# Half of pi filled last on VectorE, and the second k's read issued behind the operation that uses it

## The chip, the cores and the metric

The kernel runs on one core of a Trainium2 chip. The metric is device time in microseconds (us) of one execution; the times before are 218.34 us as the median of three runs (217.97 to 221.09). A core has five engines with an instruction queue each, executed in order: TensorE (PE, with PEld for its weight loads), VectorE (DVE), ScalarE (ACT), GpSimd (POOL) and SyncE (SP). ScalarE, GpSimd and SyncE also issue DMA transfers, which 16 DMA engines carry out.

## The reference

An attention block without softmax, followed by a token-mixing block.

```python
def phi(x):                                   # r = 8
    a = np.einsum('rd,bhsd->bhsr', S1, x)
    b = np.einsum('rd,bhsd->bhsr', S2, x)
    return np.einsum('bhsi,bhsj->bhsij', a, b).reshape(*x.shape[:-1], r * r)
q_p, k_p = phi(q), phi(k)                     # q, k, v: (4, 4, 1088, 32)
kv = np.einsum('bhsf,bhsd->bhfd', k_p, v)
z = np.sum(k_p, axis=2)
x = (q_p @ kv) / (q_p . z + 1e-06)            # heads joined: (4, 1088, 128)
...
theta = x @ w_theta
zr, zi = x * np.cos(theta), x * np.sin(theta)
y = einsum('ts,bsd->btd', w_tok_r, zr) + einsum('ts,bsd->btd', w_tok_i, zi)
u = x + y
return u + np.maximum(u @ w_ch, 0.0)
```

Here `@` and `.` in the line of `x` stand for the two einsums of the reference over the features. S1, S2 and the weights come as 64-bit numbers, and the kernel makes 32-bit numbers of them on chip.

## The kernel before

The work is cut into about 1,020 numbered operations, each a few instructions of one engine. The numbers are given in the order in which the program creates the operations; `ORDER` is a list, written out, of the order in which they are issued to their engines, and `STARTS` holds for each entry of `ORDER` a planned start in hundredths of a us. The starts decide only which buffer of a class is reused and how many idle matmuls (`spin`) TensorE runs between two operations. Each engine works through its own operations in this order; waits on semaphores between engines follow from the data.

A batch b has one read of k, q and v each (576 KB). The reads of k for b = 0 and 1 are issued by ScalarE (L668), all others by SyncE (L671), as are the rows of w_tok (L642, 1088 KB each), the small matrices S1 and S2 (`st`, L444 and L446) and a second copy of k for b = 1 to 3 (L714). Every read's completion is counted on one of eight counters, which are given to the reads in turn; a read whose counter is in use waits for the read that had it before.

What the start consists of, with the numbers that the change touches:

- 0 and 1: GpSimd fills `idle`, TensorE runs 39 idle matmuls.
- 2: VectorE fills the constants `halfpi`, `hm`, `bdm` and `ones` (`constants`, L414 to L422). They are used at different times: `halfpi` (half of pi in each partition, the bias that makes a sine a cosine) by operation 3 and then by L1203 from 54 us on.
- 3: ScalarE takes the sine of `halfpi` into `warm` (L433). The result isn't used; the sine's table is loaded by it ahead of need.
- 4 and 5: VectorE clears `st`, SyncE reads S1 and S2 into it. ScalarE (L459) and VectorE (the first L383 and L386) unpack them to `sp`; the scales, the block matrices `sbk` and the sketches of everything come from it.
- 29: ScalarE's read of k for b = 0 (k0). 32: ScalarE's read of k for b = 1 (k1), the "second k". 34, 33: SyncE's reads of k for b = 3 and b = 2. 30: SyncE's read of q for b = 0 (q0).
- ScalarE squares each k as it lands (L693, with an accumulated sum), VectorE rounds it (L383) and takes the rest (L379), TensorE transposes it (L790), and ScalarE copies the transposes out of PSUM (L793).

After the sketches, the rows of w_tok are unpacked (ScalarE L643 and L645, VectorE L383 and L379), the chain of small scales runs, and from about 57 us TensorE mixes tokens (L399 big,zs): b = 0 and 1 row by row, b = 2 and 3 together in seven products instead of eight.

In the order before, ScalarE's queue begins with the reads of k0 and k1, then the table load and `warm`, then the square of k0.

Of the kernel before, what the change touches and what calls it, by code (L numbers as in the profile page):

```python
# [31 lines left out]
RPS = 4  # L32
EARLY = (2, 60.0, 4.0)
ORDER = (
    29, 32, 4, 2, 5, 0, 1, 3, 34, 30, 356, 50, 33, 102, 44, 96, 6, 108, 103, 36, 7, 51, 366, 54, 144, 8, 97, 10, 9,
    11, 55, 109, 20, 52, 12, 57, 139, 58, 59, 60, 61, 62, 63, 126, 13, 31, 132, 56, 98, 127, 264, 14, 391, 128, 143,
    245, 15, 145, 64, 65, 67, 68, 78, 35, 69, 16, 70, 19, 148, 149, 150, 151, 152, 268, 99, 66, 79, 246, 53, 80, 100,
    110, 129, 17, 133, 130, 357, 25, 361, 81, 270, 83, 18, 203, 358, 359, 71, 41, 153, 104, 271, 210, 197, 351, 257,
# [39 lines left out]
    1013, 1007, 934, 938, 1014, 935, 1015, 939, 1016, 1017, 1018, 940, 1019, 941, 942, 943,  # L78
)
STARTS = (  # L80
    73, 73, 90, 92, 103, 130, 170, 220, 358, 404, 449, 458, 493, 510, 538, 546, 566, 579, 580, 584, 594, 612, 628,
    666, 802, 678, 693, 694, 706, 716, 719, 732, 752, 771, 798, 811, 812, 813, 815, 817, 819, 821, 823, 838, 830, 944,
    871, 899, 904, 918, 957, 967, 1088, 998, 1026, 1061, 1064, 1066, 1111, 1113, 1115, 1129, 1129, 1408, 1142, 1145,
    1155, 1164, 1168, 1170, 1172, 1174, 1176, 1225, 1236, 1251, 1251, 1260, 1271, 1299, 1303, 1313, 1319, 1327, 1334,
# [228 lines left out]
def kernel(  # L313
# [56 lines left out]
    V, A, G, T, SY = nc.vector, nc.scalar, nc.gpsimd, nc.tensor, nc.sync  # L370

    def fixed(shape, dt, name):
        b = Buf(None, shape, dt, name)
        n = math.prod(shape) * WORD[dt]
        b.ap = view(const.tile([P, (n + 3) // 4], F32, tag=name, name=name), shape, dt)
        return b
# [33 lines left out]
    halfpi = fixed((1,), F32, "halfpi")  # L410
    warm = fixed((1,), F32, "warm")

    def constants():
        V.memset(halfpi(), math.pi / 2.0)  # L414
        V.memset(hm(), 0.0)
        for h in range(H):
            V.memset(hm()[h * D:(h + 1) * D, h:h + 1], 1.0)
        V.memset(bdm(), 0.0)
        for h in range(H):
            j = h % 2  # L420
            V.memset(bdm()[j * 64:(j + 1) * 64, h:h + 1], 1.0)
        V.memset(ones(), 1.0)  # L422

    idle = fixed((GW,), BF16, "idle")
    nowhere = buf("ps", (GW,), F32, "nowhere")
# [4 lines left out]
    op("G", 0.3, lambda: G.memset(idle(), 0.0), [idle], [], due=-20.0)  # L430
    first = op("P", 3.2, lambda: [spin(112) for _ in range(39)], [nowhere], [idle], due=-10.0)
    op("V", 1.25, constants, [hm, bdm, halfpi, ones], [])
    op("A", 1.5, lambda: A.activation(warm(), halfpi(), AF.Sin), [warm], [halfpi], due=0.0)  # L433

# [1109 lines left out]
```

## Time and profile before

| what | value |
|---|---|
| runs | 217.97, 218.34, 221.09 us |
| profiled execution | 217.81 us, of which the instruction span is 215.9 us |
| busy, share of the span | PE 97%, PEld 71%, DVE 81%, ACT 53%, POOL 28% |
| chain that ended last | PE 63%, DMA 18%, ACT 14% |
| granted TensorE clock | 0.995 |
| DMA | 37.09 MB, mean 172 GB/s; 422 GB/s from 8 to 16 us |
| DMA share, 4 to 49 us | 1.02 |
| ScalarE's L668, issue to landing | 3.8 and 5.1 us |

Busy time is the time in which an engine executed something; a matmul's end is modelled, so a busy TensorE is not one at its peak. The chain is followed back from the last instruction, at each step to what released it. The DMA share is the mean busy share of the 16 DMA engines; it can pass 1 because packets overlap. A row of the timeline has start, duration, engine (with q for an instruction that only issues or waits), line, operation and tiles, and in brackets the idle time before it with what ended that.

### The profile page before, as it was taken

The page shows a single profiled execution, that of the slowest core. Times are in us where ns is not written, and L with a number is a line of the kernel's source. Part 1 is how long each engine was busy: PE and PEld are TensorE (multiplying, and loading weights), DVE is VectorE, ACT ScalarE, POOL GpSimd, SP SyncE. Part 2 cuts the span into 40 slices and gives each one's busy share as a digit, 9 for nine tenths or more (in the row PEclk, how much of TensorE's full clock was granted, in tenths as well). Part 3 has the DMA queues.
Part 4 walks back from the last instruction along what each step waited for, and adds up shares of the span by engine and source line. Part 5 has one row for each costly group of instructions (what it writes and reads, how often), then busy time and mean ns, then how long its engine had stood idle before and what let it go on. Part 6 is the DMA issues. An engine that isn't in the chain of part 4 may idle for free.

```text
span 215.9 us, 5832 instructions
## 1 busy us (share of the span) xinstructions
PE 208.9 (97%) x2396; PEld 152.8 (71%) x2396; DVE 174.3 (81%) x343; ACT 114.5 (53%) x256; POOL 59.7 (28%) x105
## 2 busy tenths in 40 slices
PE   7899999999999999999999999999999999999992
PEld 7677798868866666866668666667677776666781
DVE  1799998999999998999999798885994747456263
ACT  4899989999998895798704233363810000000000
POOL 1272740306400000604004100000006489950403
PEclk9999999999999999999999999999999999999998
DMA  6999999995998993192002402424050420010735
GB/s 222 395 418 419 384 365 420 425 315 97 360 285 267 416 432 145 75 308 45 0 0 32 74 3 112 114 109 112 2 88 15 67 39 0 0 23 8 125 55 103
DMA packets 28046, 37.09 MB, mean 172 GB/s; under 512 B 20564, under 2 KB 23044, under 8 KB 25844
## 3 DMA queue, kind: packets, MB, share of 16 engines
q1 hardware_dynamic: 22868, 31.86, 42.4%
q0 software_dynamic: 1552, 3.25, 7.2%
q10 hardware_dynamic: 3600, 1.62, 2.8%
q8 instruction: 19, 0.31, 0.6%
q14 instruction: 7, 0.06, 0.1%
HBM read 29.84 MB, written 4.00 MB: 157 GB/s over the span
## 4 chain that ended last, share of the span: by engine, by line
PE 63%; DMA 18%; ACT 14%; issue 2%; SPq 1%; DVE 1%; POOL 1%; POOLq 0%; ACTq 0%
PE ps L399 61%; DMA zs<-w_tok 13%; DMA big<-k_l 5%; ACT big L645 4%; ACT big L643 3%; ACT lv L1056 1%; PE ps L1131 1%; ACT big L1021 1%; ACT g L1199 1%; ACT g L1202 1%; ACT g L1205 1%; ACT g L1203 1%; POOL out L1299 1%; SPq L671 0%; ACT g L1135 0%
## 5 line engine op out<-in xcount | busy, mean ns | idle before, releaser
L399 PE MATMUL ps<-big,zs 128*128 128x384 f32 (+2 forms) x380 | 110.5, 436 | 0.0
L399 PEld LDWEIGHTS ps<-big,zs 128*128 128x128 f32 x380 | 66.9, 190 | 32.5
L379 POOL TENSOR_TENSOR big<-big,big 128x544 f32<-128x544 f32 x16 | 22.1, 1458 | 48.6 <-DVE big L379 44.6
L399 PE MATMUL ps<-big,big 128*32 128x32 f32 (+2 forms) x352 | 22.8, 234 | 0.0
L643 ACT ACTIVATE big<-zs 128x1088 f32<-128x1088 f32 x17 | 20.9, 1231 | 1.5 <-DMA zs<-w_tok 0.9
L379 DVE CUSTOM_DVE_ANT_0 big<-big,big 128x2176 uint16<-128x2176 uint16 x17 | 21.5, 1275 | 0.0
L645 ACT ACTIVATE big<-zs 128x1088 int32<-128x1088 uint32 (+1 forms) x18 | 21.4, 1194 | 0.3 <-DMA zs<-w_tok 0.3
L1338 ACT COPY big<-ps 80x256 f32<-80x256 f32 x1 | 0.4, 368 | 39.6 <-DMA out<-g 39.6
L399 PEld LDWEIGHTS ps<-big,big 128*32 128x32 f32 (+1 forms) x352 | 15.3, 124 | 6.8 <-issue 0.8
L1276 ACT COPY g<-ps 128x384 f32<-128x384 f32 (+1 forms) x6 | 2.5, 466 | 23.4 <-PE ps L399 23.4
L379 DVE TENSOR_TENSOR big<-big 128x544 f32<-128x544 f32 x8 | 9.5, 1204 | 5.6 <-PE ps L399 5.6
L383 DVE TENSOR_SCALAR big<-big 128x1088 int32<-128x1088 int32 x17 | 12.2, 719 | 0.0
L379 POOL TENSOR_TENSOR mf<-mv,sm 128x32 f32<-128x32 f16 (+1 forms) x3 | 0.8, 262 | 39.1 <-DVE sm L379 39.1
L428 PE MATMUL ps<-idle 128*128 128x112 bf16 (+1 forms) x67 | 10.0, 312 | 1.3 <-POOL idle L430 1.3
L379 DVE TENSOR_TENSOR g<-lv 128x768 f32<-128x768 f32 x12 | 11.1, 950 | 0.1
L399 PEld LDWEIGHTS ps<-w,big 128*128 128x128 f32 (+1 forms) x76 | 9.8, 189 | 1.4
L379 DVE TENSOR_TENSOR big<-big,hf 128x1152 f32<-128x1152 f32 x8 | 10.7, 1351 | 0.0
L399 PE MATMUL ps<-w,big 128*128 128x128 f32 (+1 forms) x76 | 10.5, 278 | 0.0
L399 PE MATMUL ps<-sbk,g 128*128 128x64 f32 x72 | 10.0, 276 | 0.3 <-ACT g L793 0.3
L379 DVE TENSOR_TENSOR zs<-zs,g 128x384 f32<-128x384 f32 (+2 forms) x24 | 9.8, 447 | 0.2
L386 DVE SCALAR_TENSOR_TENSOR big<-ps,even,big 128x384 f32<-128x384 f32 (+1 forms) x10 | 4.8, 493 | 6.3 <-PE ps L399 6.2
L1199 ACT ACTIVATE g<-ps 128x384 f32<-128x384 f32 x12 | 5.9, 504 | 7.3 <-PE ps L399 7.3
(199 smaller groups left out, 379.2 us busy)
## 6 DMA issues: line engine op xcount, KB each, us to landing
zs<-w_tok SPq DMA_DIRECT2D x17, 1088.0 KB, 10.6
big<-k_l SPq DMA_DIRECT2D x5, 576.0 KB, 13.2
big<-v_l SPq DMA_DIRECT2D x4, 576.0 KB, 15.6
big<-q_l SPq DMA_DIRECT2D x3, 576.0 KB, 10.7
big<-hf POOLq DMA_DIRECT2D x3, 576.0 KB, 10.0
far<-zs SPq DMA_DIRECT2D x3, 576.0 KB, 2.8
zs<-far SPq DMA_DIRECT2D x12, 144.0 KB, 4.3
big<-k_l ACTq DMA_DIRECT2D x2, 576.0 KB, 4.4
```

Source lines behind the costliest of these rows:

```text
L379: eng.tensor_tensor(out=o, in0=a, in1=b, op=f)
L383: (eng or V).tensor_scalar(out=o, in0=a, scalar1=s1, scalar2=s2, op0=op0, **kw)
L386: (eng or V).scalar_tensor_tensor(out=o, in0=a, scalar=s, in1=b, op0=op0, op1=op1)
L399: T.matmul(o, lhs, rhs, start=start, stop=stop, skip_group_check=True)
L428: T.matmul(nowhere()[:, :n], idle()[:, 0:P], idle()[:, :n], start=True, stop=True, skip_group_check=True)
L643: op("A", 0.22 + n * 0.0009, lambda: A.activation(dfn(), words_of(raw(), n)[1].bitcast(F32), AF.Prelu, scale=2.0**-112, alpha=-(2.0**32)), ...
L645: op("A", 0.22 + n * 0.0009, lambda: A.activation(stp(), words_of(raw(), n)[0].bitcast(U32), AF.Copy, scale=2.0**-29), [stp], [raw])
L1021: op("A", act(GW) + 0.1, lambda g=g, tr=tr: A.activation(f()[:, g * GW:(g + 1) * GW], tr(), AF.Copy, scale=s()[:, 0:1]), [(f, g)], [tr, (s ...
L1056: op("A", act(480), lambda g=g, lp=lp: A.copy(lv().rearrange("p l (c n) -> p l c n", n=HR)[:, :, g * GC:(g + 1) * GC], lp().rearrange("p c ...
L1131: T.transpose(tr()[:, i * P:(i + 1) * P], qp()[:, i * H + 2 * n:i * H + 2 * n + 2].rearrange("p h i j -> p (h i j)"), ident())
L1199: op("A", act(GW), lambda cs=cs, th=th: A.activation(cs()[:, 0], th(), AF.Copy, bias=ROUND), [(cs, 0)], [th])
L1276: op("A", act(w), lambda: A.copy(u(), yp()[:, :w]), [uT], [yp])
```

## The change

In `constants`, the fill of `halfpi` goes from the first place to the last, behind the fill of `ones`. In `ORDER`, operation 32 (the read of k1) goes from behind 29 to behind 3, so that on ScalarE it stands behind the table load and the operation on `halfpi`; `STARTS` is shifted with it (32 has now 220 instead of 73). No instruction is added or removed.

```diff
 ORDER = (
-    29, 32, 4, 2, 5, 0, 1, 3, 34, 30, 356, 50, 33, ...
+    29, 4, 2, 5, 0, 1, 3, 32, 34, 30, 356, 50, 33, ...
 STARTS = (
-    73, 73, 90, 92, 103, 130, 170, 220, 358, ...
+    73, 90, 92, 103, 130, 170, 220, 220, 358, ...
     def constants():
-        V.memset(halfpi(), math.pi / 2.0)
         V.memset(hm(), 0.0)
         for h in range(H):
             V.memset(hm()[h * D:(h + 1) * D, h:h + 1], 1.0)
...
         V.memset(ones(), 1.0)
+        V.memset(halfpi(), math.pi / 2.0)
```

In the built program ScalarE's instructions then begin: read of k0, table load, sine of `halfpi` (which waits for VectorE), read of k1, square of k0. VectorE's fills have `halfpi` last. TensorE's, GpSimd's and SyncE's instructions keep their order. Two counters change hands: the read of k1 now counts on the one that SyncE's read of q0 had, and q0 on the one that k1 had. So SyncE's read of the first v (8.57 us in the timeline) waits for q0 instead of k1, and its third row of w_tok (9.64 us) for k1 instead of q0.

## The prediction

> **What bounds the kernel now.** I read the page first (busy shares, the slices, the chain that ended last), then the timeline of the first 14 us, in which all edited instructions lie, then the DMA queues by window, and last the stretch in which an early shift would have to survive.
>
> ```profile
> PE 208.9 (97%) x2396; PEld 152.8 (71%) x2396; DVE 174.3 (81%) x343; ACT 114.5 (53%) x256; POOL 59.7 (28%) x105
> DMA  6999999995998993192002402424050420010735
> ```
>
> The page: TensorE is the long pole, and the DMA engines are full over the first nine slices (5.4 us each). By stage (the table of windows): DMA share 1.02 from 4 to 49 us, with ScalarE busy 24.7 of 27.6 us and then 16.7 of 17.4; from 49 us on TensorE is busy all the time to the end. A shift of the start changes the span only if it reaches TensorE at about 49 us.
>
> The timeline of the start (start, duration, engine and line; in brackets idle time and what ended it):
>
> ```profile
> 0.72 0.88 ACTq L668 DMA_DIRECT2D big<-k_l  x2
> 0.90 0.06 DVE L414 MEMSET halfpi<- 128x1 f32 x1
> 0.98 0.74 SPq L444 DMA_DIRECT2D st<-s_t  x1
> 1.63 1.28 ACT L433 ACT_TABLE_LOAD   x1 [1.63 <-PEq L1534]
> 1.99 0.17 DVE L422 MEMSET ones<- 128x128 f32 x1
> 2.27 0.38 SPq L671 DMA_DIRECT2D big<-k_l  x1
> 2.92 0.20 ACT L433 ACTIVATE warm<-halfpi 128x1 f32<-128x1 f32 x1
> 4.56 1.17 ACT L693 ACTIVATE big<-big 128x1152 f32<-128x1152 f32 x1 [1.44 <-DMA big<-k_l]
> 6.37 0.24 ACT L459 ACTIVATE sp<-st 128x48 f32<-128x48 f32 x1 [0.55 <-DMA st<-s]
> 6.65 0.19 DVE L383 TENSOR_SCALAR sp<-sp 128x48 int32<-128x48 int32 x1 [4.49 <-ACT sp L459]
> 8.20 0.33 SPq L714 DMA_DIRECT2D big<-k_l  x1
> 8.42 1.18 ACT L693 ACTIVATE big<-big 128x1152 f32<-128x1152 f32 x1
> ```
>
> Two reads gate the start: k0 (4.56) and the small st (6.37), for which VectorE idles 4.49 us. The second k is first used at 8.42, by the second L693. The DMA queues from 1.2 to 4.8 us, then from 4.8 to 6.4 (packets, MB, share):
>
> ```profile
> q10 hardware_dynamic: 229, 0.98, 80.3%
> ...
> q1 hardware_dynamic: 208, 0.29, 64.7%
> q10 hardware_dynamic: 59, 0.20, 32.5%
> ```
>
> q10 is ScalarE's queue, q1 is SP's. st was issued at 0.98 to 2.22, yet q1 moved nothing until 4.8: the engines served k0 and k1 (1.18 MB) first. So reads are served about in the order in which they arrive, and st stands behind k1.
>
> The chain of waits later on (start, length, what), and the ScalarE row at its joint:
>
> ```profile
> 15.22 16.38 DMA zs<-w_tok
> ```
>
> ```profile
> 31.63 1.23 ACT L643 ACTIVATE big<-zs 128x1088 f32<-128x1088 f32 x1 [0.58 <-DMA zs<-w_tok]
> ```
>
> ScalarE is ready at 31.05 and waits 0.58 us for a row of w_tok that went through the full queue for 16 us.
>
> **The change, part by part.** (a) VectorE. The 0.06 us fill of halfpi goes from second to last of the fills: ready at about 2.2 (ones ends at 2.16) instead of 0.96. The other fills move up by at most 0.06. Cost 0; VectorE idles 4.49 us behind it, and without that cover the same fills would take the same time in another order.
>
> (b) ScalarE. With one read's issue less ahead, the table load starts at about 1.2 (1.63 less the second issue, 0.45), ends at 2.5, and warm runs then: halfpi at 2.2 is hidden by the table load. Warm ends about 0.4 earlier, in front of 1.44 us of idle. Cost 0. Without the table load the late halfpi would hold ScalarE from 1.2 to 2.2, still inside that idle time.
>
> (c) The issue of k1 (1.15 in before) now stands behind warm. Lower bound: when warm's wait for halfpi is over, 2.2. Upper bound: shortly after warm starts; the only row in which ScalarE issues right behind an operation is this pair, 0.13 us from start to issue, before the copy ends:
>
> ```profile
> 211.77 0.37 ACT L1338 COPY big<-ps 80x256 f32<-80x256 f32 x1 [39.55 <-DMA out<-g]
> 211.90 0.38 ACTq L1299 DMA_DIRECT2D out<-g  x1
> ```
>
> That gives 2.5 + 0.13 = 2.6. I take 2.4: 1.25 us later than before. Behind it on ScalarE stands only L693 on k0, which waits for k0's landing (4.56) anyway.
>
> (d) Landing. Before: k0 4.5, k1 at the latest 6.2 (1.15 plus 5.1, the longer of the two times to landing of L668), st 6.3, SP's first k (fourth of the kernel) 8.2, q0 9.6 (the SP issues at 8.20 and 9.64 wait for these two). Now the order of arrival is k0, st, then k1 and SP's first k, issued within 0.3 us of each other (2.27 to 2.65 on SP). st loses one read of 590 KB ahead of it: 0.59 MB / 0.42 MB per us (the rate of 8 to 16 us) = 1.4, so it lands at about 4.9. The set up to SP's first k is the same bytes as before, so its last read lands at 8.2 again: k1 at 6.8 if it goes first, 8.2 if the two share, 9.6 if q0 (issued at 2.69) comes in ahead too. I take 7.8, between the first two.
>
> The Trainium skill ("DMA: Bandwidth & Descriptors", section "Queues, rings and completion order") says that each DMA engine takes the queues in turn, a packet at a time. The trace disagrees for the first 4.8 us, where one queue had all the service; taken strictly, the rule would have let st in beside k0, and k1 would share from its arrival and land by about 8, with which the sum stays and the starved rival below falls away; as the trace disagrees at this very place, I leave that rival its chance.
>
> (e) What gets earlier. L459 can run when L693 on k0 ends (5.63 + 0.19 = 5.82) instead of 6.37: 0.55 earlier. VectorE's unpacking and ScalarE's short row (copies L793, L700, L701) follow, so the second L693 could start at 8.42 - 0.55 = 7.87; k1 at 7.8 does not hold it. With k1 at 8.2 it starts 0.2 earlier than before, with k1 at 9.6 1.2 later.
>
> (f) Where that gain goes. ScalarE would come to L643 at 30.5 instead of 31.05 and wait there for the row of w_tok. That row is bound by bytes through a queue that is full from 3 us on, and no byte is taken out; it lands at 31.6. ScalarE has 0.7 us of slack in the next 17.4 and TensorE 0.4, so from there all runs as before. Gain 0.
>
> (g) The DMA engines' own loss. k0 was issued at 0.72, and the rate was 0.08 to 0.28 MB/us until 3.0 and 0.39 to 0.42 after: 2.3 us from issue to full rate. k0 and st now run out at about 4.3, and reads issued at 2.3 to 2.4 reach full rate at 4.6 to 4.7. Bounds: 0.4 lost, or 0.4 gained if st's small packets slip into the slow ramp (in 4.8 to 6.4 us the mean was 308 GB/s instead of 420, which is 0.4 us). I take 0.15 lost; it goes straight into 31.6.
>
> (h) Counters. In the built program SP's read of the first v (8.57) now waits for q0's counter instead of k1's, so it is issued at 9.6; the third row of w_tok (9.64) waits for k1. The reads behind them on SP move by up to 1.0 us, up to the one at 12.28. The queue hides that: a read of v takes 15.6 us from issue to landing at the median, nearly all of it behind others. If the queue ran dry it would cost 1.0.
>
> Sum: 0 + 0 + 0 + 0.15 = +0.15 us on the profiled execution's 217.81 (span 215.9 and 1.9 around it), 217.96. The median of the runs shown is 0.53 higher, 218.34, so 218.5 there.
>
> **The rivals.** *Late k1* (slower). q0 and a share of the next row go ahead of k1, it lands at 9.6 to 10 and the second L693 waits: 1.2 to 1.6 late, and ScalarE, which is dense (8 to 16 us: 7.87 of 8), carries it to 31.6, where 0.58 is given back, and a further 0.2 in TensorE's idle time near 37 and 43 us. +0.4 to +0.8: 219.0. For it: q0's issue is only 0.3 behind mine. Against: half the estimate of (c) lies ahead of SP's first k.
>
> *Starved k1* (the other side: slower than before, from one mechanism). If a queue that comes late waits until the other queue's fetched reads are done, as this read on GpSimd's queue did,
>
> ```profile
> big<-hf POOLq DMA_DIRECT2D x3, 576.0 KB, 10.0
> ```
>
> k1 lands at 2.4 + 10.0 = 12.4, the second L693 is 4.0 late, 0.8 is given back: +3.2, 221.6. It decides from a landing past 9.2 on (8.42 and the 0.8). Against: at 2.4 us SP's queue holds only st and one k, and the read of that row also adds into its target.
>
> The Trainium skill ("TensorE: Matmul & The Clock Gate", section "Part 1: The HAM clock gate") adds that TensorE idle for a window of some 3.4 us falls to half clock. No row here shows it (the granted clock is 1.00 in every window to 80 us); in this rival TensorE would idle from about 8.5 to 12.5, and by the rule the next 3.4 us would run at half speed, another 1.7: about 223.3.
>
> *The early start survives* (faster). If the row at 31.6 comes earlier as well (st in the ramp, 0.4), 0.55 - 0.15 of (e) gets through: 217.9. For it: L459's row is real idle time. Against: (f).
>
> *The text of the change does nothing*: k1's slack (landed 6.2, used 8.42) swallows the later issue, and st gains nothing: 218.3.
>
> **How the numbers follow.** Forecast with the last rival, whose times can't be told apart: 0.60; late k1 0.22; starved 0.08; early start 0.10. The predicted time is 218.5. The range has to take in 0.4 of (g) and the early start below, late k1 with its 0.8, and part of the starved case above, beside executions that spread from 217.97 to 221.09: 217.5 to 220.7. Two per cent is 4.4 us, about what a measurement of this kernel can tell from no change; only the starved case with all that hangs on it reaches that, and nothing on the fast side comes near: faster 0.02, same 0.91, slower 0.07.
>
> **What would show it.** After: warm at about 2.5 with no idle time before it; ScalarE's second issue of L668 at 2.2 to 2.6; L459 at about 5.8 without a wait for st; VectorE's first L383 near 6.1; the second L693 at 7.9 to 8.2; the wait before L643 near 31.6 longer than 0.58. Wrong if the second L693 waits for k1 beyond 9.2, if L643 starts before 31 or after 32.2, or if st still lands at 6.3.

## The result, and the profile after

The changed kernel takes 219.38 us (median of 22 executions), the kernel before 218.12 us beside it: a ratio of 1.0064, 95% interval 1.0049 to 1.008. That is inside the range and inside 2%, as forecast, but it is a real small loss, and the mechanism forecast did not happen: the second k came late, which was one of the rivals. All ratios are to the kernel before, run beside each, and leave out disturbed executions, so a ratio need not be that of the two medians. The profiled execution of the changed kernel is a long one, 221.15 us (span 219.2, granted clock 0.984); others had a clock of 1.0 and 218.37 to 219.76 us, so the lines below are to be read together with a second profile further down.

The page (busy time, and the granted TensorE clock in 40 slices of 5.5 us):

```profile
PE 211.4 (96%) x2396; PEld 154.8 (71%) x2396; DVE 174.8 (80%) x343; ACT 114.2 (52%) x256; POOL 57.5 (26%) x105
PEclk9958999999999999999999999999999999999999
```

PE has 2.5 us more of busy time for the same 2,396 instructions, and the clock, full in every slice of the start before, falls in the third and fourth.

The timeline of the start (start, duration, engine and line; idle time and what ended it in brackets):

```profile
0.72 0.38 ACTq L668 DMA_DIRECT2D big<-k_l  x1
1.14 1.28 ACT L433 ACT_TABLE_LOAD   x1 [1.14 <-PEq L1534]
2.08 0.06 DVE L422 MEMSET halfpi<- 128x1 f32 x1
2.19 0.35 ACTq L668 DMA_DIRECT2D big<-k_l  x1
2.43 0.20 ACT L433 ACTIVATE warm<-halfpi 128x1 f32<-128x1 f32 x1
4.55 1.16 ACT L693 ACTIVATE big<-big 128x1152 f32<-128x1152 f32 x1 [1.91 <-DMA big<-k_l]
5.71 0.23 ACT L459 ACTIVATE sp<-st 128x48 f32<-128x48 f32 x1
10.18 1.16 ACT L693 ACTIVATE big<-big 128x1152 f32<-128x1152 f32 x1 [2.30 <-DMA big<-k_l]
10.20 0.88 PE L790 MATMUL ps<-ident,big 128*128 128x128 f32 x6 [1.77 <-DMA big<-k_l]
10.35 0.33 SPq L714 DMA_DIRECT2D big<-k_l  x1
```

Up to L459 all stands as predicted: halfpi, the table load, warm, the issue of the second k at 2.19, L459 without its wait for st. Then the second k is missing: the second L693 waits 2.30 us and starts at 10.18 (8.42 before), and TensorE stands idle for 1.77 us. SP's L714, whose wait ended at 8.20 before, goes at 10.35.

The DMA queues from 1.2 to 4.8 us, then from 4.8 to 10.2 (packets, MB, share):

```profile
q10 hardware_dynamic: 169, 0.71, 65.7%
q1 hardware_dynamic: 153, 0.04, 6.1%
...
DMA packets 413, 1.83 MB, mean 339 GB/s; under 512 B 43, under 2 KB 43, under 8 KB 382
...
q1 hardware_dynamic: 294, 1.36, 69.6%
q10 hardware_dynamic: 119, 0.47, 27.5%
```

The second k (all that q10, ScalarE's queue, still has) shares the engines with SP's q1, and the mean is 339 GB/s; in the same stretch of the kernel before it was 384. The difference is largest from 4 to 8 us (all packets, then q10; before, then after):

```profile
DMA packets 501, 1.47 MB, mean 369 GB/s; under 512 B 185, under 2 KB 185, under 8 KB 501
q10 hardware_dynamic: 138, 0.54, 33.8%
...
DMA packets 395, 1.07 MB, mean 268 GB/s; under 512 B 166, under 2 KB 166, under 8 KB 395
q10 hardware_dynamic: 122, 0.49, 40.0%
```

The engines' share fell only from 1.00 to 0.89 there, the rate from 369 to 268: a packet of q10 also took longer, 0.21 us on the mean against 0.16 (the share of 16 engines' 4 us, over the packets). Counted in bytes from 0 to 12 us, before and then after:

```profile
DMA packets 935, 3.80 MB, mean 317 GB/s; under 512 B 228, under 2 KB 228, under 8 KB 807
```

```profile
DMA packets 844, 3.35 MB, mean 279 GB/s; under 512 B 217, under 2 KB 217, under 8 KB 737
```

0.45 MB are missing, which at 0.42 MB per us are 1.07 us of service. This profile is at the upper end: five later ones have the same start up to the second k (e7, e13, e12, e4 and e6 below), and they miss 0.44, 0.34, 0.23, 0.22 and 0.15 MB. The windows of TensorE from 8 to 12, 12 to 16 and 16 to 20 us (busy, granted clock, DMA share, GB/s):

```profile
8.00:12.00 4.00, 2.15 (x42) 0.93 1.01 415
12.00:16.00 4.00, 4.00 (x105) 0.50 1.02 413
16.00:20.00 4.00, 4.00 (x27) 0.72 1.00 418
```

Behind the idle time the clock stands at 0.50. In finer windows it does so from 11.4 to 18.3 us. ScalarE reaches the row of w_tok that it waited for at 31.63 only at 34.43, and waits no more:

```profile
34.43 1.23 ACT L643 ACTIVATE big<-zs 128x1088 f32<-128x1088 f32 x1
```

So three things are late in this execution: the second k, the bytes behind it, and TensorE by its clock. The experiments try to take them apart.

### The profile page after: what moved, and what is told of

Same layout as the page of the kernel before. It is cut to its first block, busy times and chain, and to the rows that moved or that the text cites. A ratio compares the mean times of both kernels' runs of the same rounds, so it can differ in the third digit from the quotient of the medians.

```text
span 219.2 us, 5833 instructions
## 1 busy us (share of the span) xinstructions
PE 211.4 (96%) x2396; PEld 154.8 (71%) x2396; DVE 174.8 (80%) x343; ACT 114.2 (52%) x256; POOL 57.5 (26%) x105
## 4 chain that ended last, share of the span: by engine, by line
PE 93%; DMA 4%; POOL 0%; ACT 0%; issue 0%; DVE 0%; POOLq 0%; ACTq 0%
PE ps L399 84%; DMA big<-k_l 4%; PE ps L428 2%; PE ps L1131 2%; PE ps L1018 2%; PE ps L790 2%; POOL out L1299 0%; ACT L433 0%; PE ps L1189 0%; POOLq L1540 0%; PE ps L973 0%; DVE g L1303 0%; PE ps L963 0%; ACTq L668 0%; DVE big L379 0%
## 5 line engine op out<-in xcount | busy, mean ns | idle before, releaser
L643 ACT ACTIVATE big<-zs 128x1088 f32<-128x1088 f32 x17 | 20.9, 1229 | 0.6 <-DVE lv L379 0.6
L428 PE MATMUL ps<-idle 128*128 128x112 bf16 (+1 forms) x67 | 10.5, 317 | 1.3 <-POOL idle L430 1.3
L399 PE MATMUL ps<-sbk,g 128*128 128x64 f32 x72 | 11.3, 300 | 0.0
L399 PEld LDWEIGHTS ps<-sbk,g 128*128 128x128 f32 x72 | 10.4, 215 | 0.3
## 6 DMA issues: line engine op xcount, KB each, us to landing
zs<-w_tok SPq DMA_DIRECT2D x17, 1088.0 KB, 10.2
big<-q_l SPq DMA_DIRECT2D x3, 576.0 KB, 11.4
```

What stands on the lines that cost most here:

```text
L399: T.matmul(o, lhs, rhs, start=start, stop=stop, skip_group_check=True)
L428: T.matmul(nowhere()[:, :n], idle()[:, 0:P], idle()[:, :n], start=True, stop=True, skip_group_check=True)
L643: op("A", 0.22 + n * 0.0009, lambda: A.activation(dfn(), words_of(raw(), n)[1].bitcast(F32), AF.Prelu, scale=2.0**-112, alpha=-(2.0**32)), ...
```

## The experiments

**The two halves of the change.** *e1_pi_first*: the changed kernel without the move of the fill, so that the second k's read still stands behind warm, but halfpi is ready at 0.96.

```diff
     def constants():
+        V.memset(halfpi(), math.pi / 2.0)
         V.memset(hm(), 0.0)
...
-        V.memset(halfpi(), math.pi / 2.0)
```

> Half of pi stays the first fill; only the read of the second k goes behind ScalarE's operation. Theory A (what counts is when the read of k1 reaches the DMA engines, against SP's reads): ScalarE's queue goes on as soon as the operation's wait for half of pi is met, at 0.96, while the table load still runs, so L668's second issue is at about 1.15 to 1.2, k1 lands at 6.2 as before, the second L693 starts at 8.4 without a wait: ratio 1.000 (0.998 to 1.002). Rival (the read waits for the table load, wherever half of pi stands): second issue at 2.4, k1 lands near 10, the wait of 2.3 us before L693 is there again: ratio 1.006.

217.97 us, ratio 1.0012 (0.9989 to 1.0035). The start of its timeline:

```profile
1.15 1.28 ACT L433 ACT_TABLE_LOAD   x1 [1.15 <-PEq L1534]
1.22 0.38 ACTq L668 DMA_DIRECT2D big<-k_l  x1
```

The issue goes while the table load runs: what holds it in the changed kernel is warm's wait for halfpi alone. The second L693 starts at 8.38. This kernel has the changed order of reads and with it the exchanged counters; neither costs anything that shows.

*e2_pi_last*: the other half, the fill last and the reads as before.

```diff
     def constants():
-        V.memset(halfpi(), math.pi / 2.0)
         V.memset(hm(), 0.0)
...
+        V.memset(halfpi(), math.pi / 2.0)
```

> Only the fill of half of pi goes last; both reads of k stay at the head of ScalarE's queue. Theory A: both issues of L668 at 0.72 and 1.15, the operation on half of pi at 2.9 as before, nothing else moves: ratio 1.000 (0.998 to 1.002). Rival (the late fill itself costs): ratio 1.003 to 1.006 with a wait of ScalarE for VectorE in front of warm.

218.28 us, ratio 1.0013 (0.9992 to 1.0034); warm at 2.93 as before. Neither half costs anything that can be measured (the intervals end at 1.0035); the loss is in their coming together.

These two profiles also measure something that the others need. L643 in e1, then in e2:

```profile
30.90 1.24 ACT L643 ACTIVATE big<-zs 128x1088 f32<-128x1088 f32 x1
...
31.01 1.24 ACT L643 ACTIVATE big<-zs 128x1088 f32<-128x1088 f32 x1
```

ScalarE comes there as in before (31.05), but the row of w_tok has landed already, where before it waited to 31.63. SP issued this row at 14.63 and 13.51 instead of 15.22. So one profile's L643 can differ by 0.6 to 0.7 us from another's with no cost behind it, and 31.63 is a late value.

**How late is too late.** *e5_pi_mid*: the changed kernel with the fill in the third place.

```diff
         for h in range(H):
             V.memset(hm()[h * D:(h + 1) * D, h:h + 1], 1.0)
+        V.memset(halfpi(), math.pi / 2.0)
...
-        V.memset(halfpi(), math.pi / 2.0)
```

> The changed kernel with half of pi filled third of the constants (behind the fill of hm and its heads) instead of last, and ScalarE's read of the second k still behind ScalarE's operation on the table. Its issue is then expected at about 1.4 to 1.6 us, between the 0.72 of before and the 2.19 of the changed kernel. Theory: what counts is whether the second k's packets are under way when the first k runs out at about 4.3 us (2.3 us from issue to full rate). Issued at 1.5 they are, so there is no dip in the rate, the second k lands by about 7 and the second square does not wait: ratio to before 0.998 to 1.002. Rival: any read of ScalarE's queue that is issued behind SP's first reads takes turns with them. Then the second k lands later than 8.4, the second square waits, and the ratio is 1.003 or more.

218.49 us, ratio 1.0009 (0.9979 to 1.0039). Issue, second L693, and the joint at L643:

```profile
1.52 0.34 ACTq L668 DMA_DIRECT2D big<-k_l  x1
8.58 1.17 ACT L693 ACTIVATE big<-big 128x1152 f32<-128x1152 f32 x1
31.87 1.22 ACT L643 ACTIVATE big<-zs 128x1088 f32<-128x1088 f32 x1 [0.74 <-DMA zs<-w_tok]
```

No wait at the second L693, in line with what was expected. But the rate still dipped: 3.63 MB by 12 us, 0.17 less than before, and L643 0.24 later, which is less than two profiles can differ. The changed start, with its issue at 2.19 or 2.20, misses 0.15 to 0.45 MB, so the bytes alone do not separate the two; the second k does, which is in time here and late in all six of those profiles (second L693 at 8.98 to 10.18).

**Queue or time.** *e3_one_queue*: the second k's read goes to SP's queue, behind st and ahead of SP's first k, so at the same time as in the changed kernel but with no second queue.

```diff
-    29, 32, 4, 2, 5, 0, 1, 3, 34, 30, 356, ...
+    29, 4, 2, 5, 32, 0, 1, 3, 34, 30, 356, ...
...
-        if b < 2 and nm == "k":
+        if b < 1 and nm == "k":
```

> Half of pi first; the read of k1 is issued by SP, behind st and ahead of SP's first k, so that one queue has k0 and the other all else in one order. Theory A: st lands at 4.9 as in the changed kernel, k1 behind it at 6.5 to 7.2 with no other queue to take turns with, L459 at 5.7 and the second L693 at 7.7 to 7.9 without a wait; that start is 0.6 earlier than before, and by the prediction's step on the row of w_tok near 31.6 it is lost in a longer wait there: ratio 0.999 to 1.001. Rival (the early start survives): ratio 0.996 to 0.998. Rival (any k1 behind st is late): L693 waits until 10, ratio 1.006.

218.86 us, ratio 1.0055 (1.0026 to 1.0084), above what I expected. Its ScalarE rows:

```profile
5.86 0.23 ACT L459 ACTIVATE sp<-st 128x48 f32<-128x48 f32 x1
7.89 1.18 ACT L693 ACTIVATE big<-big 128x1152 f32<-128x1152 f32 x1
32.11 1.22 ACT L643 ACTIVATE big<-zs 128x1088 f32<-128x1088 f32 x1 [1.52 <-DMA zs<-w_tok]
```

This is the start that the prediction described: the second L693 at 7.89 without a wait, 0.53 earlier than before, and the whole gain lost in a longer wait at L643, whose row lands 0.48 later in this profile (less than two profiles can differ). The second k, issued at 2.28 on SP, is in time when only the rest of the first k stands in the other queue. Where the loss of 0.55% comes from stays open: the trace has TensorE waits of 0.59 at 38 and 0.53 at 79 us that before has not, but e2, which costs nothing that shows, has one of 0.97 at 79. With it stays open how much of the changed kernel's 0.64% belongs to the late second k, since this kernel loses about as much without one.

*e11_k_ahead_of_st*: the kernel before with SP's first k issued at the very start, beside ScalarE's first (`STARTS` as before).

```diff
-    29, 32, 4, 2, 5, 0, 1, 3, 34, 30, 356, ...
+    29, 32, 34, 4, 2, 5, 0, 1, 3, 30, 356, ...
```

> The kernel before with SP's first k issued ahead of SP's small reads st, at about 0.98 instead of 2.27, while ScalarE's queue has the first and second k from 0.72 and 1.15. It puts two large reads of two queues side by side at the very start. If the DMA engines take the two queues in turns, the first k lands 0.5 to 1.2 us later than before (first square at 5.0 to 5.8 instead of 4.56) and the second k after 7. If they serve in the order in which reads arrive, the first square starts at 4.5 to 4.7. Either way st stands behind one more large read, so L459 moves from 6.37 to 7.2 or later and the second square to 9 or later: ratio 1.000 to 1.004.

219.28 us, ratio 1.0015 (0.9985 to 1.0045). The first L693, and the queues from 1.2 to 4.8 us:

```profile
6.37 1.17 ACT L693 ACTIVATE big<-big 128x1152 f32<-128x1152 f32 x1 [3.21 <-DMA big<-k_l]
...
q1 hardware_dynamic: 105, 0.48, 46.7%
q10 hardware_dynamic: 98, 0.45, 36.1%
```

Both reads are issued at 0.72, and the engines serve the two queues about evenly; the first k lands 1.8 us later than before. My reading "about in the order in which they arrive" is refuted for reads that stand side by side. Sharing by itself costs no rate: from 4.8 to 10.2 us this kernel moved 425 GB/s, and by 12 us 3.95 MB, 0.15 more than before.

The whole start is late here (second L693 at 10.31, L643 at 32.82 without a wait), though no byte is. Its median is 0.95 above that of the kernel before beside it (218.33), but the interval of its ratio takes in no loss at all. It decides nothing on what lateness costs.

**Which lateness costs.** *e7_after_again* and *e13_after_third*: the changed kernel unaltered.

> The changed kernel unaltered, beside the others on this chip. Both theories: ratio 1.005 to 1.008, the second k landing between 9 and 10.2, executions with a clock of 1.0 at 218.4 to 219.7 and some at 0.984 near 221.

> The changed kernel unaltered, on the same chip as the six idle matmuls. Theory and rival: 3 to 5 of 12 executions with a clock below 0.992; median 219.2 to 219.6; ratio 1.004 to 1.007.

219.46 us, ratio 1.0042 (1.0011 to 1.0072), and 219.40 us, ratio 1.0051 (1.0021 to 1.0082). The profile of e7_after_again has a clock of 1.00 from 8 to 20 us and shows the loss without its effect:

```profile
9.71 1.17 ACT L693 ACTIVATE big<-big 128x1152 f32<-128x1152 f32 x1 [1.71 <-DMA big<-k_l]
9.73 0.88 PE L790 MATMUL ps<-ident,big 128*128 128x128 f32 x6 [1.18 <-DMA big<-k_l]
32.76 1.22 ACT L643 ACTIVATE big<-zs 128x1088 f32<-128x1088 f32 x1 [0.47 <-DMA zs<-w_tok]
```

L643 is 1.13 later than before (31.63), and 1.75 later than in e2. ScalarE came 1.24 later than before (32.29 against 31.05), the row 1.13 later. In e13 ScalarE finds its row landed, at 32.45. The first L1189, a TensorE marker at 53.0 in before, stands at 54.2 here, and at 56.1 in the profile with the low clock.

*e9_square_late*: the kernel before, with ScalarE's square of the second k done one and a half times more; no transfer changes.

```diff
+            def square():
+                if b == 1:
+                    A.activation(flat(r()), kc(), AF.Square)
+                    A.activation(flat(r())[:, 0:n // 2], kc()[:, 0:n // 2], AF.Square)
+                A.activation(flat(r()), kc(), AF.Square, accum_out=km()[:, 1:2])
```

> The kernel before with the second square (ScalarE, the second k) done one and a half times more ahead of the real one, 1.17 + 0.6 us of ScalarE work with no other effect: the lateness of the second square in the changed kernel's trace (1.76 us), without any change to a transfer. Theory that ScalarE's lateness is what costs: it comes to the read row at 31.6 about 1.2 us late after the 0.58 of wait, so plus 1.0 to 1.2 us, ratio 1.005. Rival, that the bytes which the DMA engines did not move between 4 and 8 us (0.45 MB, about 1.05 us) are what costs: then ScalarE's own lateness mostly disappears further on, ratio 1.000 to 1.002.

220.03 us, ratio 1.006 (1.0031 to 1.009). The square is 1.99 late (10.41), and L643:

```profile
32.84 1.25 ACT L643 ACTIVATE big<-zs 128x1088 f32<-128x1088 f32 x1
```

1.21 late, without a wait. ScalarE's lateness is enough for a loss of this size. It is more of it, though, than the changed kernel has with a full clock (1.99 against 1.29 at the square, 1.79 against 1.24 on coming to L643), so this does not say that all of the changed kernel's loss is ScalarE's.

*e10_extra_bytes*: the kernel before, with 0.44 MB more on SP's queue behind q0.

```diff
+            if b == 0 and nm == "q":
+                SY.dma_start(extra[:], k[0].rearrange("p c h d -> p (c h d)")[:, 0:864])
```

> The kernel before with one more read on SP's queue, issued right behind the first q: 0.44 MB of the first k, written to a spare DRAM buffer that nothing reads. That is the service which the DMA engines lost by 12 us in the changed kernel (3.35 MB against 3.80), given away without making the second k late. Theory that the lost service costs by itself: the row of w_tok behind L643 (31.63 in before) lands 0.44 / 0.42 = 1.05 us later, ScalarE waits for it from 31.05 to 32.7, and the time rises by 0.9 to 1.1 us: ratio 1.004 to 1.005, with the second square still at 8.4 to 8.6. Rival, that only ScalarE's and TensorE's lateness at the second k counts: ratio 1.000 to 1.002. A copy into DRAM may take more or less service than one on the chip; the landing of the row at L643 tells.

219.14 us, ratio 1.0028 (0.9998 to 1.0058). The second square at 8.41 as before, and the joint (L643 is L644 here):

```profile
32.60 1.22 ACT L644 ACTIVATE big<-zs 128x1088 f32<-128x1088 f32 x1 [1.14 <-DMA zs<-w_tok]
```

0.97 late, with the row last (expected 1.05); ScalarE itself came 0.41 later than before. By time the interval reaches from nothing to more than was expected, so that the bytes cost by themselves is not shown. In these profiles each of the two moves the joint by about what both together do: they meet at L643, where the later one counts. By these numbers mending one alone would gain little; that is argued from single profiles, whose L643 can differ by 0.6 to 0.7 us, and was not run.

**The clock.** *e4_spins*, the changed kernel again, was meant to fill TensorE's idle time with ten idle matmuls.

```diff
             def trs(g=g, tr=tr):
+                for _ in range(10 if b == 1 and g == 0 else 0):
+                    spin()
```

> The changed kernel with ten idle matmuls more (some 1.6 us) on TensorE ahead of the transposes of k1, where it stood idle for 1.8 us. Theory A with the clock as a second part: the wait of ScalarE for k1 stays at 2.3 us, the granted clock stays at 1.00 in every execution, the slowest executions (221 us and more, clock 0.984) are gone: ratio 1.004 to 1.005. Rival (the clock has no part in it): ratio 1.0064 as for the change, with the same spread. If the ten matmuls cost more than they cover, TensorE starts the transposes later than 10.2 and the ratio is above 1.007.

223.56 us, ratio 1.0194 (1.0144 to 1.0243). They ran in the wrong place:

```profile
25.60 1.78 PE L428 MATMUL ps<-idle 128*128 128x384 bf16 x10
```

The group numbered 0 is the last of the second k's in the planned order. In a dense stretch they cost their 1.78 us and more, and the run says nothing on the gap. *e6_spins_at_wait* puts nine ahead of the group that runs first, and *e12_six_spins* six in the same place.

```diff
             def trs(g=g, tr=tr):
+                for _ in range(9 if b == 1 and g == 1 else 0):
+                    spin()
```

> The changed kernel with nine idle matmuls (1.6 us in all) on TensorE right ahead of the first transposes of the second k, in the place where TensorE idled 1.8 us. Theory: the lateness of the second k costs about 1.0 us by itself, and the fall of the granted clock behind the idle time costs the rest in the executions that show it. With the gap filled no execution shows a clock below 0.995, all lie within 218.2 and 219.6, median about 219.0, ratio 1.004. Rival: the clock falls for another reason, such as the weaker supply of work between 10 and 16 us: then executions at 0.984 and 221 us remain, in about the share of the changed kernel (4 of 22 at 0.984, 8 of 22 below 0.992).

> The changed kernel with six idle matmuls (1.1 us) instead of nine ahead of the first transposes of the second k: they end before the second k lands, so that they cannot push TensorE's own work, and leave at most 0.7 us of idle time there. Theory that the idle time of 1.2 to 1.8 us lets the clock fall in part of the executions: at most 1 of 12 below 0.992, and the median about 219.1, a little under the changed kernel. Rival, that the clock's fall has another cause: 3 to 5 of 12 below 0.992, as in the changed kernel (11 of 34 so far).

219.71 us, ratio 1.0077 (1.0048 to 1.0105), and 219.78 us, ratio 1.0057 (1.0031 to 1.0084): no better than the changed kernel, against what I expected. With nine, TensorE's transposes start at 9.96 though the second k was there at 9.26. Granted clocks below 0.992: the changed kernel 15 of 46 executions, the kernel before 3 of 109, the two kernels with the gap filled 3 of 23. That the changed kernel has more of them is shown; that the gap at 8.4 is where they come from is suggested by its profile and not shown by these counts. Two kernels without a late second k have them as well: e3 3 of 12, and e9, in which ScalarE alone is late, 5 of 12. So a source further on, which all of these share, stands as a rival. One of the three is the profiled execution of e12_six_spins, and its fall is elsewhere (TensorE windows 80.5 to 81 and 84 to 84.5 us, and the wait ahead of them):

```profile
79.99 0.25 PE L399 MATMUL ps<-sq,sm 32*32 32x16 f32 x8 [1.26 <-ACT sm L852]
...
80.50:81.00 0.50, 0.50 (x9) 0.57 1.03 435
...
84.00:84.50 0.50, 0.50 (x3) 1.00 0.87 366
```

Half clock for about 3.4 us, behind 1.26 us of idle time.

## Why the prediction was right, and where it was wrong

The median was to stay within 2% and inside 217.5 to 220.7, and did. The mechanism forecast did not happen; *late k1* did. That the number fell inside is owed to the range, which had taken late k1 in, and not to the sum: it had +0.15 us, and the median rose by 1.26.

- **(a), (b), (c) right.** The fill at 2.08, the table load at 1.14, warm at 2.43, the issue at 2.19 (taken 2.4, lower bound 2.2). e1 shows why the lower bound was the place: the issue waits for halfpi and not for the table.
- **(d) is the step that failed.** st came as said. The second k was to land at 7.8, at the latest at 9.6; it was used at 10.18, at 9.71 and 9.78 in the two repeats, and at 8.98 to 9.26 in the three kernels with idle matmuls, which have the same start. The sum rested on "the set up to SP's first k is the same bytes as before, so its last read lands at 8.2 again": that wait of SP ended at 10.35. The bytes were the same, the rate was not.
- **(g) is the same error as a term.** 0.15 us of lost service was taken, 0.4 the bound; 1.07 us were lost by 12 us, and 0.36 to 1.05 in the five other profiles of this start. I let every read reach full rate 2.3 us after its issue. With the first k out and the late reads coming up in two queues, the engines stayed at 268 GB/s from 4 to 8 us (369 before; 269 to 337 in the five others). e10 prices such a loss at 0.97 at L643 in its one profile, and by time not clearly.
- **(e) half right.** L459 at 5.71 against the 5.82 forecast, VectorE's unpacking with it. The second L693 was not 0.55 earlier but 1.76 later, 1.29 in e7.
- **(f) right in its outcome, weak in its reason.** e3 has the early start without a late k, and the gain ends in a wait of 1.52 at L643. But the row is not bound to land at 31.6: it was there by 30.90 and 31.01 in e1 and e2, with no more bytes moved by 12 us than in before.
- **(h) too small, and harmless.** The first v was issued at 11.61, not at 9.6; the DMA share was 1.00 or more from 8 to 31.6 us, so it was hidden. In e1, with the same counters and the second k in time, it went at 10.01, at no cost that shows.
- **The rivals.** Late k1 was given 1.2 to 1.6 of lateness and a cost of 0.4 to 0.8. With a full clock the lateness was 1.29, and the cost at L643 was 1.13: it gave back 0.58 once, but forgot that the row itself would be late as well, and that the 0.58 is not there in every execution. By time, the executions with a clock of 0.992 or more have a median of 219.03, 0.9 above before; the median of all is 0.35 higher. In the repeats e7 and e13 the same difference is nothing and 0.23, so what the clock adds to the median is small and not settled.
- **The clock** was named only with the starved rival, at 4 us of idle time. It fell here behind 1.77.

The Trainium skill ("DMA: Bandwidth & Descriptors", section "Queues, rings and completion order") has each DMA engine take the queues in turn. I set that aside on the strength of st's wait; e11, with 105 and 98 packets side by side, agrees with it. By the prediction's estimate the rule alone would have put the second k at about 8 here, and the runs have it at 9.0 to 10.2, so it does not give the lost rate.

## What to carry to other kernels

A read that is moved behind a wait can cost more than its delay (e1, e5 and the changed kernel move the same read; only the last, with the longest delay, loses by it): ask what the DMA engines have left to do when the reads ahead of it run out, and count bytes up to a fixed time rather than assume the full rate. Slack computed for a transfer (landed 6.2, used 8.42) holds only while the reads around it stay the same; a delay of 1 us put the read beside SP's (2.19 against 2.27 and 2.67) and cost 2.8 to 4 us of landing. Where two late things meet at one wait, price each alone before mending either, and compare more than one profile: the row at L643 landed 0.6 us apart in starts that were alike.

## What the runs showed of the hardware

- ScalarE issues a DMA while its table load runs (1.22 inside 1.15 to 2.43), if the wait ahead of it in the queue is met.
- Two reads issued together in two queues are served evenly, at full rate once both are under way (e11: 425 GB/s). A small read issued 0.26 us behind a large one of the other queue need not be: st in before moved nothing until 4.8 us. What decides between the two ways of service, and why late reads in two queues came up so slowly (268 to 337 GB/s from 4 to 8 us in six profiles, against 353 in one queue, e3), the runs leave open: the trace does not tell the 16 engines apart.
- A high busy share is not yet the full rate: 0.89 went with 268 GB/s and 1.00 with 369 from 4 to 8 us, 1.03 with 415 in e11.
- TensorE's clock halves behind idle times of 1.26 and 1.77 us in some executions (the changed kernel, e12) and stays full behind 1.18 and 1.32 in others (e7, e11). It did so for 3.4 us in one case (80.6 to 84.0) and 6.8 in the other (11.4 to 18.3). The Trainium skill ("TensorE: Matmul & The Clock Gate", section "Part 1: The HAM clock gate") gives a window of some 3.4 us that runs freely: the lengths agree with one and two windows, and a free window would explain why only some executions are hit. That it takes a whole idle window, these runs do not bear out.
